# A fused 2-D DFT and squared-ReLU feed-forward kernel: the third TensorE pass of 49 pair steps replaced by arithmetic on VectorE

## The chip, the cores and the metric

The kernel runs on one core of a Trainium2 chip. The metric is device time in microseconds (us), from runs of the whole kernel on the chip; lower is better. The profile is one execution of the kernel, taken by the hardware profiler.

## The reference

For each of 8 batches the real part of a two-dimensional DFT over a 3008 x 256 array is taken, and every one of the resulting 24064 rows goes through a two-layer network with a squared ReLU.

```python
X = np.fft.fft(x, axis=1)          # x: (8, 3008, 256) float32
X = np.fft.fft(X, axis=2)
a = X.real.reshape(24064, 256)
h = np.maximum(a @ w_in, 0.0)      # w_in: (256, 2048)
out = (h * h @ w_out)              # w_out: (2048, 256), float32
```

## The kernel before

The real part of the DFT is a sum of a cosine product and a sine product, and the rows k and S-k of one batch differ only in the sign of the sine product. So the kernel computes one column for each such pair of rows: with P = gh[0]^T zc (cosine) and Q = gh[1]^T zs (sine), the row k has the hidden value P+Q and the row S-k has P-Q. The DFT over the 256 features is folded into the first weight matrix: `gh` holds, for 128 values of d, the cosine part (`gh[:, 0]`), the sine part (`gh[:, 1]`) and the "turn" part (`gh[:, 2]`), all 2048 hidden features wide. Partition 0 of `zs` and of `gh[:, 1]` is used for something else: it holds the row d = 128, which belongs to the cosine product and keeps its sign. `turn2` (L328 to L330) is therefore -2 on partitions 1 to 127 and 0 on partition 0, and `gh[:, 2]` is `gh[:, 1]` times `turn2` (L448): adding gh[2]^T zs to P+Q gives P-Q with the row d = 128 kept.

The 12040 columns are cut into 25 windows w of up to 512 columns (`wins`). Windows 6 to 23 have 512 columns each. In a window there are eight pair steps s = 0 to 7, one for every two groups of 128 hidden features:

- `pq(s)` (L680 to L685): four matmuls of 512 columns, which put P+Q of two groups in a PSUM tile `ph` (two of these tiles exist).
- `square(s, 0)` (L692 to L696): ScalarE takes ReLU of `ph` into an SBUF tile `h1` (three exist), VectorE multiplies it by itself into the left half of `h2`.
- `others(s)` (L698 to L709): the jobs that are spread over the steps. These are 16 matmuls of 256 columns of the second layer for the window before (`part`, L587 to L618, whose PSUM result ScalarE copies to `osb` in every odd step, and the SP queue then stores), the work that prepares later windows, and matmuls that make `zc` and `zs` of the next window (`z_steps`, L458; their last part, `minus` at L494, is on VectorE).
- `turn(s)` (L687 to L690): two matmuls of 512 columns, which add the turn part to the same PSUM tile, so that it then holds P-Q.
- `square(s, 1)`: ReLU and square again, columns reversed, into the right half of `h2`.

The program is written in the order in which each engine is to work: every engine takes its instructions in order. The second layer of window w is done in window w+1: its step s does column group s of `h2`, over all 16 groups of hidden features.

Some windows carry the folding of one more batch of x (`fold_at`): windows 5, 8, 10, 13, 16 and 19. There the steps 0 to 4 each hold one or several VectorE jobs, in this order: `d_even` (L348 to L350), `n_cos` (L358), `d_odd` (L353, after which GpSimd loads the next batch), `n_sin` (L361), `odds` (L368, which writes `od`). In step 5, behind the second layer's matmuls, comes `nyq` (L370 to L375): two tiny TensorE matmuls that read `od`, and a VectorE copy. Step 6 has `even`, step 7 `back`. The windows 6, 9, 12, 15, 18 and 21 (`late_at`) have four smaller VectorE jobs in their steps 2 to 5 (L404, L415).

The loop that orders a window is this:

```python
for s0 in range(0, NST, ng):
    ss = range(s0, s0 + ng)
    for s in ss: pq(s)
    for s in ss: square(s, 0)
    others(s0)
    for s in ss: turn(s)
    for s in ss: square(s, 1)
    for s in ss[1:]: others(s)
```

where `ng` is 1 in all windows but two early ones.

Of the kernel before, what the change touches and what calls it, by code (L numbers as in the profile page):

```python
# [8 lines left out]
F32 = mybir.dt.float32  # L9
F16 = mybir.dt.float16  # L10
I32 = mybir.dt.int32
AF = mybir.ActivationFunctionType
ALU = mybir.AluOpType

HS = 32.0
P = 128
# [3 lines left out]
def rev_dim(ap, i):  # L20

    dims = [list(d) for d in ap.ap]
    step, cnt = dims[i]
    dims[i] = [-step, cnt]
    return bass.AP(tensor=ap.tensor, offset=ap.offset + step * (cnt - 1), ap=dims)
# [3 lines left out]
def kernel(  # L29
# [14 lines left out]
    nc = tc.nc  # L44
    B, S, D = x.shape
    _, F = moe_w_in.shape
# [7 lines left out]
    NFC = F // P  # L54
    WN = 512

    FIRST = [240, 512, 376, 376, 512, 448]
    R23 = float(2.0 ** 23)

    RQ = (1, 3, 5, 0, 2, 4)  # L60

# [11 lines left out]
    wins = []  # L73
# [5 lines left out]
    NW = len(wins)  # L79

    def win_of(col):
        return max(w for w in range(NW) if wins[w][0] <= col) if col < TOT else NW
# [17 lines left out]
    const = ctx.enter_context(tc.tile_pool(name="const", bufs=1))  # L100
    tmp = ctx.enter_context(tc.tile_pool(name="tmp", bufs=2))
# [8 lines left out]
    ps_h = ctx.enter_context(tc.tile_pool(name="ps_h", bufs=2, space=bass.MemoryType.PSUM))  # L110
    ps_o = ctx.enter_context(tc.tile_pool(name="ps_o", bufs=2, space=bass.MemoryType.PSUM))
# [56 lines left out]
    perm = [const.tile([P, P], F16, name=f"perm{i}") for i in range(2)]  # L168
# [3 lines left out]
    nc.gpsimd.memset(idx["c"][0:2, :], P - 3)  # L172
    idx["f"] = iota([P, 1], [[1, 1]], -1, 1, "idx_f")
    nc.gpsimd.memset(idx["f"][0:1, :], 0)
    w16 = [const.tile([P, 2, F // 2], F16, name=f"w16_{i}") for i in range(2)]
    for i in range(2):
        nc.gpsimd.dma_start(out=w16[i], in_=moe_w_in[:, i * F // 2 : (i + 1) * F // 2].rearrange("(c p) f -> p c f", p=P))
    wout16 = const.tile([P, NFC, D], F16, name="wout16")
# [2 lines left out]
    def small(shape, name):  # L181
        return const.tile(shape, F32, name=name)
# [22 lines left out]
    def table_steps(e):  # L205
# [19 lines left out]
        def args(h):  # L225
            t = st["t", h] = tmp.tile([P, 3, NE], F32, name="t", tag="tt")
            for j in range(nr):
                r = row(h, j)
                if e == 0:
                    nc.scalar.activation(t[:, j, 0:n], st["kf"], AF.Copy, bias=R23, scale=vs[:, r : r + 1])  # L230
                else:
                    nc.vector.tensor_scalar(out=t[:, j, 0:n], in0=st["kf"], scalar1=vs[:, r : r + 1], scalar2=R23, op0=ALU.mult, op1=ALU.add)

        def turns(h):
            t = st["t", h]
            nc.vector.tensor_scalar(out=t[:, 0:nr, 0:n], in0=t[:, 0:nr, 0:n], scalar1=-R23, scalar2=-float(S), op0=ALU.add, op1=ALU.mult)

# [44 lines left out]
    at = const.tile([P, 2, P + 1], F32, name="at")  # L282
    for c in range(2):
        nc.scalar.activation(at[:, c, :], drow, AF.Copy, bias=R23, scale=dvs[:, c : c + 1])
    nc.vector.tensor_scalar(out=at, in0=at, scalar1=-R23, scalar2=-float(D), op0=ALU.add, op1=ALU.mult)
    for c in range(2):
# [141 lines left out]
    gh = const.tile([P, 3, F], F16, name="gh")  # L428
# [17 lines left out]
    def gh_turn(cc):  # L446
        f0 = cc * 512
        nc.vector.tensor_scalar(out=gh[:, 2, f0 : f0 + 512], in0=gh[:, 1, f0 : f0 + 512], scalar1=turn2[:, 0:1], scalar2=None, op0=ALU.mult)  # L448
# [3 lines left out]
    def zwin(w):  # L452
        if w not in zc:
            zc[w] = zp.tile([P, WN], F16, name="zc", tag="zc")
            zs[w] = zp.tile([P, WN], F16, name="zs", tag="zs")
        return zc[w], zs[w]
# [101 lines left out]
    for cc in range(1, F // 512):  # L558
        gh_turn(cc)

    def store(osb, p0, g0, m, minus, eng=nc.sync):

        for b, k0, kstep, n, c0 in runs:
            il, ih = max(g0, c0) - c0, min(g0 + m, c0 + n) - 1 - c0
            if minus and k0 in (0, H):
                il = max(il, 1)
            cnt = ih - il + 1
            if cnt <= 0:
                continue
            if minus:  # L570
                lo = p0 + (m - 1) - (c0 + ih - g0)
                row = b * S + S - (k0 + kstep * ih)
            else:
                lo = p0 + c0 + il - g0
                row = b * S + k0 + kstep * il
            eng.dma_start(
                out=bass.AP(tensor=out.tensor, offset=out.offset + row * D, ap=[[kstep * D, cnt], [1, D]]),
                in_=osb[lo : lo + cnt, :])
# [46 lines left out]
    def spread(jobs, i, n):  # L625
        return jobs[len(jobs) * i // n : len(jobs) * (i + 1) // n]
# [3 lines left out]
    def fold_jobs(i):  # L630
        f = folds[i] = fold_steps(i)
        return [f["d_even"], f["n_cos"], f["d_odd"], f["n_sin"], f["odds"], f["nyq"], f["even"], f["back"]]

    fold_at, late_at = {}, {}
    for i in range(2, B):
        fold_at[win_of(col_of[i, 0]) - 2] = i
        late_at[win_of(col_of[i, 1]) - 2] = i
    NST = NFC // 2
    old = None
    for w in range(NW):  # L640
        g0, wn = wins[w]
        h2 = h2p.tile([P, NFC, 2 * WN], F16, name="h2", tag="h2")
        zcw, zsw = zwin(w)

        lo, hi = 0, NST - 1
        at = [[] for _ in range(NST)]
        post = [[] for _ in range(NST)]
        if w == 0:
            at[2] = [f0s["even"], f0s["back"]]
        elif w == 1:  # L650
            fj = fold_jobs(1)
            at = [[f] for f in fj[0:5]] + [[], [], []]
            post[5] = fj[5:6]
            lo, hi = 6, 7
        elif w == 2:
            te = table_steps(1)
            at = [[folds[1]["even"], lambda: te["freq"](), lambda: te["args"](0)], [lambda: te["turns"](0)], [lambda: te["mods"](0)],
                  [lambda: te["absm"](0)], [lambda: te["sins"](0)], [lambda: te["coss"](0)], [], [lambda: te["weigh"]()]]
            for st in range(4):
                at[st + 3] = at[st + 3] + f0s["late"][st : st + 1]  # L660
            at[7].append(folds[1]["back"])
        elif w in fold_at:
            fj = fold_jobs(fold_at[w])
            at = [[f] for f in fj[0:5]] + [[], fj[6:7], fj[7:8]]
            post[5] = fj[5:6]
        elif w == win_of(col_of[1, 1]) - 1:
            for st in range(4):
                at[st] = folds[1]["late"][st : st + 1]
            lo = 4
        if w in late_at:  # L670
            for st in range(4):
                at[st + 2] = at[st + 2] + folds[late_at[w]]["late"][st : st + 1]
        zj, zl = [], []
        for u in need[w + 1]:
            zu = z_steps(u)
            zj += [(zu, 0, 0), (zu, 1, 0), (zu, 0, 1), (zu, 1, 1)]
        f2 = ffn2_steps(*old) if old else []
        phs = {}

        def pq(s):  # L680
            ph = phs[s] = ps_h.tile([P, 2, 512], F32, name="ph", tag="psh")
            for a in range(2):
                f0 = (2 * s + a) * P
                nc.tensor.matmul(ph[:, a, 0:wn], gh[:, 0, f0 : f0 + P], zcw[:, 0:wn], start=True, stop=False)  # L684
                nc.tensor.matmul(ph[:, a, 0:wn], gh[:, 1, f0 : f0 + P], zsw[:, 0:wn], start=False, stop=True)  # L685

        def turn(s):  # L687
            for a in range(2):
                f0 = (2 * s + a) * P
                nc.tensor.matmul(phs[s][:, a, 0:wn], gh[:, 2, f0 : f0 + P], zsw[:, 0:wn], start=False, stop=True, skip_group_check=True)  # L690

        def square(s, sg):  # L692
            h1 = h1p.tile([P, 2, 512], F16, name="h1", tag="h1")
            nc.scalar.activation(h1[:, :, 0:wn], phs[s][:, :, 0:wn], AF.Relu)  # L694
            hv = rev_dim(h1[:, :, 0:wn], 2) if sg else h1[:, :, 0:wn]
            nc.vector.tensor_tensor(h2[:, 2 * s : 2 * s + 2, sg * wn : (sg + 1) * wn], hv, hv, op=ALU.mult)  # L696

        def others(s):  # L698
            for j in at[s]:
                j()  # L700
            for j in spread(f2, s, NST):
                j()
            for j in post[s]:
                j()
            if s == lo:
                zl[:] = [j for zu, part, h in zj for j in zu(part, h)]
            if s >= lo:
                for j in spread(zl, s - lo, hi - lo) if s < hi else []:
                    j()  # L709


        ng = 2 if w == 0 or wins[w - 1][1] < 384 < wn else 1
        for s0 in range(0, NST, ng):
            ss = range(s0, s0 + ng)
            for s in ss:
                pq(s)
            for s in ss:
                square(s, 0)
            others(s0)
            for s in ss:  # L720
                turn(s)
            for s in ss:
                square(s, 1)
            for s in ss[1:]:
                others(s)
        old = (w, h2)
# [32 lines left out]
```

## Time and profile before

| | |
|---|---|
| median of 3 runs | 633.91 us (633.72 to 635.05) |
| span of the profiled execution, first to last instruction | 632.0 us |
| TensorE busy (matmul) | 615.9 us |
| ScalarE busy | 457.4 us |
| VectorE busy | 369.5 us |
| GpSimd busy | 76.5 us |
| granted TensorE clock, mean | 1.000 |
| matmuls of `pq` and `turn` on 512 columns | 3 x 320 |
| VectorE squares on 128 x 1024 (L696) | 320, mean 692 ns |
| ScalarE ReLU on 128 x 1024 (L694) | 320, mean 1026 ns |

"Busy" is the time in which an engine had at least one instruction in work. Matmuls follow each other in a pipeline, so the duration of one (379 ns on 512 columns) is more than the distance between the starts of two. In the table of groups, the last columns give the idle time of the engine just before these instructions and what ended it. The SP queue issues the stores; the GpSimd queue issues the loads of x and of the fold.

### The profile page before, as it was taken

Reading aid. Unit: us, or ns where it says so; the run is one execution under the profiler, and the core shown is the slowest. Engines: PE = TensorE matmul, PEld = TensorE weight load, DVE = VectorE, ACT = ScalarE, POOL = GpSimd, SP = SyncE. Lnnn points to the kernel's source line nnn. Section 1 sums busy time; section 2 is a strip of 40 time slices with the busy share of each in tenths; the row PEclk is TensorE's granted clock in tenths of the full one; section 3 lists DMA queues with packets and bytes.
Section 4 is the critical chain, followed back from the end, with each engine's and each line's share of the span. In section 5 each row is a group of like instructions: output and inputs, shape, how many; then the busy total and the mean of one; then the engine's idle time right before and its main releaser. Section 6 shows DMA issues by size and latency. Waiting matters only on the chain.

```text
span 632.0 us, 11586 instructions
## 1 busy us (share of the span) xinstructions
PE 615.9 (97%) x4548; PEld 439.1 (69%) x4548; DVE 369.5 (58%) x604; ACT 457.4 (72%) x610; POOL 76.5 (12%) x125
## 2 busy tenths in 40 slices
PE   5899999999999999999999999999999999999997
PEld 2457776776777767767777677777677776777786
DVE  7887656765457557645576455854557555454430
ACT  7787778777777677767777777777777777777662
POOL 5352200022002200220011100030000200000000
PEclk9999999999999999999999999999999999999999
DMA  8936211172112711631127211262111311111112
GB/s 146 211 82 127 85 34 34 50 164 78 36 43 58 184 46 42 144 97 35 51 44 160 74 52 39 59 151 73 40 31 55 111 34 47 38 46 35 49 54 65
DMA packets 36525, 47.52 MB, mean 75 GB/s; under 512 B 4216, under 2 KB 30328, under 8 KB 36472
## 3 DMA queue, kind: packets, MB, share of 16 engines
q0 software_dynamic: 9344, 22.14, 17.6%
q1 hardware_dynamic: 26899, 24.44, 12.7%
q8 instruction: 35, 0.57, 0.4%
q10 hardware_dynamic: 228, 0.21, 0.1%
q14 instruction: 19, 0.15, 0.1%
HBM read 33.63 MB, written 27.84 MB: 97 GB/s over the span
## 4 chain that ended last, share of the span: by engine, by line
PE 93%; DVE 3%; ACT 2%; issue 1%; POOL 0%; ACTq 0%; POOLq 0%; DVEq 0%
PE po L596 51%; PE ph L684 12%; PE ph L685 12%; PE ph L690 12%; PE pz L478 4%; ACT h L694 1%; PE pw L301 1%; DVE h L696 1%; PE pg L436 0%; ACT cos L259 0%; DVE fe L349 0%; DVE fo L353 0%; ACT sin L248 0%; ACT gh L440 0%; DVE od L368 0%
## 5 line engine op out<-in xcount | busy, mean ns | idle before, releaser
L694 ACT ACTIVATE h<-ph 128x1024 f16<-128x1024 f32 (+4 forms) x400 | 368.4, 974 | 80.0 <-PE ph L690 72.1
L696 DVE TENSOR_TENSOR h<-h 128x1024 f16<-128x1024 f16 (+4 forms) x400 | 262.4, 660 | 231.6 <-ACT h L694 228.2
L596 PE MATMUL po<-wout,h 128*128 128x256 f16 (+1 forms) x3024 | 361.6, 273 | 0.0
L596 PEld LDWEIGHTS <-h 128*128 128x128 f16 (+1 forms) x3024 | 296.8, 98 | 71.3
L684 PE MATMUL ph<-zc,gh 128*128 128x512 f16 (+4 forms) x400 | 145.9, 366 | 1.1 <-ACT h L694 0.8
L685 PE MATMUL ph<-zs,gh 128*128 128x512 f16 (+4 forms) x400 | 145.9, 366 | 0.4 <-ACT zs L487 0.4
L690 PE MATMUL ph<-zs,gh 128*128 128x512 f16 (+4 forms) x400 | 112.8, 366 | 2.0 <-ACT h L694 1.5
L611 ACT ACTIVATE osb<-po 128x512 f32<-128x512 f32 (+3 forms) x95 | 54.9, 582 | 57.4 <-PE po L596 52.4
L685 PEld LDWEIGHTS <-gh 128*128 128x128 f16 x400 | 39.1, 98 | 43.8 <-issue 2.5
L684 PEld LDWEIGHTS <-gh 128*128 128x128 f16 x400 | 39.0, 98 | 41.8 <-issue 0.5
L690 PEld LDWEIGHTS <-gh 128*128 128x128 f16 x400 | 37.2, 97 | 12.7 <-issue 4.3
L421 POOL COPY xt<-xt 128x2 f16<-128x2 f16 x16 | 2.5, 186 | 173.2 <-DVE xt L404 173.2
L130 POOL DMA_INDIRECT xo<-in_x_dram,idx_r x15 | 22.1, 1471 | 4.6 <-issue 4.6
L125 POOL DMA_DIRECT2D xo<-in_x_dram x8 | 6.0, 751 | 109.8 <-DVE fo L353 109.8
L483 ACT ACTIVATE es<-pz 128x376 f32<-128x376 f32 (+1 forms) x32 | 15.4, 481 | 5.3 <-PE pz L478 5.2
L391 POOL DMA_INDIRECT rb<-scr,idx_r x16 | 18.5, 1158 | 4.9 <-issue 4.9
L487 ACT ACTIVATE zs<-pz 128x376 f16<-128x376 f32 (+23 forms) x27 | 8.5, 358 | 9.9 <-PE pz L478 9.9
L349 DVE TENSOR_TENSOR fe<-xo 128x3072 f16<-128x3072 f16 x8 | 14.3, 1786 | 1.6 <-DMA xo<-in_x_dram,idx_r 1.3
L353 DVE TENSOR_TENSOR fo<-xo 128x3072 f16<-128x3072 f16 x8 | 14.2, 1779 | 0.0
L494 DVE SCALAR_TENSOR_TENSOR zc<-es,pz 128x376 f16<-128x376 f32 (+20 forms) x26 | 9.4, 392 | 7.2 <-ACT zc L487 7.0
L301 PE MATMUL pw<-spn 128*128 128x384 f16 x30 | 8.2, 448 | 5.2 <-DVE spn L290 5.2
L389 POOL DMA_DIRECT2D rb<-scr x16 | 8.8, 551 | 33.4 <-DMA scr<-ev 33.0
(106 smaller groups left out, 220.4 us busy)
## 6 DMA issues: line engine op xcount, KB each, us to landing
out_dram<-osb SPq DMA_DIRECT2D x77, 128.0 KB
xo<-in_x_dram POOLq DMA_DIRECT2D x7, 768.0 KB, 7.0
scr<-ev POOLq DMA_DIRECT2D x8, 390.0 KB, 4.4
rb<-scr POOLq DMA_DIRECT2D x16, 130.0 KB, 5.1
out_dram<-osb SPq DMA_DIRECT2D x12, 94.0 KB
w<-in_moe_w_in_dram POOLq DMA_DIRECT2D x2, 512.0 KB, 10.0
wout<-in_moe_w_out_dram POOLq DMA_DIRECT2D x1, 1024.0 KB, 14.5
out_dram<-osb SPq DMA_DIRECT2D x8, 75.0 KB
```

The costliest lines, as they stand in the source:

```text
L130: nc.gpsimd.indirect_dma_start(out=flat(q), out_offset=None, in_=bass.AP(tensor=x.tensor, offset=0, ap=[[XW, B * S * D // XW], [1, XW]]), ...
L301: nc.tensor.matmul(pw[:, 0 : 3 * P], spn[:, 0, 0, :], spn.rearrange("p c r d -> p (c r d)")[:, 0 : 3 * P], start=True, stop=True)
L391: nc.gpsimd.indirect_dma_start(out=rb[:, q].rearrange("p r d -> p (r d)"), out_offset=None, in_=bass.AP(tensor=src.tensor, offset=src.offs ...
L478: nc.tensor.matmul(ps[:, o0:o1], lhs, tab, start=(h == 0 and k == 0), stop=last, skip_group_check=True)
L483: nc.scalar.activation(es[:, 0:n], ps[:, 0:n], AF.Copy, bias=0.0, scale=1.0)
L596: nc.tensor.matmul(po[0:m, j * D : (j + 1) * D], h2[:, fc, q : q + m], wout16[:, fc, :], start=(fc == 0), stop=(fc == NFC - 1))
L611: nc.scalar.activation(osb[0:mm].rearrange("p s d -> p (s d)")[:, lo:hi], po[0:mm, lo:hi], AF.Copy, bias=0.0, scale=HS * HS)
L684: nc.tensor.matmul(ph[:, a, 0:wn], gh[:, 0, f0 : f0 + P], zcw[:, 0:wn], start=True, stop=False)
L685: nc.tensor.matmul(ph[:, a, 0:wn], gh[:, 1, f0 : f0 + P], zsw[:, 0:wn], start=False, stop=True)
L690: nc.tensor.matmul(phs[s][:, a, 0:wn], gh[:, 2, f0 : f0 + P], zsw[:, 0:wn], start=False, stop=True, skip_group_check=True)
L694: nc.scalar.activation(h1[:, :, 0:wn], phs[s][:, :, 0:wn], AF.Relu)
L696: nc.vector.tensor_tensor(h2[:, 2 * s : 2 * s + 2, sg * wn : (sg + 1) * wn], hv, hv, op=ALU.mult)
```

## The change

In 49 of the pair steps the second pass over `zs` with the turn part is left out. These steps are s = 1, 3 and 5 in windows 6, 7, 9, 11, 12, 14, 15, 17, 18, 20, 21, 22 and 23, and s = 1 and 3 in the fold windows 8, 10, 13, 16 and 19. Such a step runs in another order:

- `half_q(s)`: the two Q matmuls alone; ScalarE copies -2Q into the tile `sn` (two exist, in the space of the weights `w16`, which are no longer used by then); VectorE makes 2 times the d = 128 row's share in two instructions, one for each group of 128 features (`eb`, which has that row of `zs` on all partitions, times `wv`, one number for each hidden feature), and adds it to `sn`.
- `others(s)`, as before.
- `half_p(s)`: the two P matmuls add to the same PSUM tile, which then holds P+Q; ScalarE copies it to the left half of a tile `hd`; VectorE adds `sn` and writes the sum, columns reversed, to the right half; VectorE takes the maximum with 0 over both halves in place, and multiplies both halves with themselves into `h2`.

`row_weights`, in step 0 of window 3, makes `wv` once: 16 matmuls with one column each, which pick partition 0 of `gh[:, 1]`, and a VectorE multiplication by 2. `row_spread(w + 1)`, at the head of step 7 of window w, is a DMA on the SP queue that copies partition 0 of `zs` of the next window to all 128 partitions of `eb` (1 KB each).

```diff
+    MANY, FEW = (1, 3, 5), (1, 3)
...
+    def row_weights():
+        pv = ps_o.tile([P, 512], F32, name="pv", tag="po")
+        for fc in range(NFC):
+            nc.tensor.matmul(pv[:, fc : fc + 1], gh[:, 1, fc * P : (fc + 1) * P], perm[0][:, P - 1 : P], start=True, stop=True)
+        nc.vector.tensor_scalar(out=wv, in0=pv[:, 0:NFC], scalar1=2.0, scalar2=None, op0=ALU.mult)
...
+    def row_spread(w):
+        wn = wins[w][1]
+        t = eb[w] = tmp.tile([P, WN], F16, name="eb", tag="kf")
+        src = zwin(w)[1][0:1, 0:wn]
+        nc.sync.dma_start(out=t[:, 0:wn], in_=bass.AP(tensor=src.tensor, offset=src.offset, ap=[list(src.ap[0]), [0, P], [1, wn]]))
...
+    def halved(w):
+        if wins[w][1] < WN or w < 6:
+            return ()
+        return FEW if w in fold_at else MANY
...
+        if w == 3:
+            at[0].append(row_weights)
...
+        def half_q(s):
+            ph = phs[s] = ps_h.tile([P, 2, 512], F32, name="ph", tag="psh")
+            for a in range(2):
+                f0 = (2 * s + a) * P
+                nc.tensor.matmul(ph[:, a, 0:wn], gh[:, 1, f0 : f0 + P], zsw[:, 0:wn], start=True, stop=True)
+            i = ROT[0] % 2
+            sn = sns[s] = const.tile([P, 2, 2, WN], F16, name=f"sn{i}", tag=f"w16_{i}")
+            nc.scalar.activation(sn[:, 0, :, 0:wn], ph[:, :, 0:wn], AF.Copy, bias=0.0, scale=-2.0)
+            for a in range(2):
+                nc.vector.tensor_scalar(out=sn[:, 1, a, 0:wn], in0=eb[w][:, 0:wn], scalar1=wv[:, 2 * s + a : 2 * s + a + 1], scalar2=None, op0=ALU.mult)
+            nc.vector.tensor_tensor(sn[:, 0, :, 0:wn], sn[:, 0, :, 0:wn], sn[:, 1, :, 0:wn], op=ALU.add)
+
+        def half_p(s):
+            ph, sn = phs[s], sns[s]
+            for a in range(2):
+                f0 = (2 * s + a) * P
+                nc.tensor.matmul(ph[:, a, 0:wn], gh[:, 0, f0 : f0 + P], zcw[:, 0:wn], start=False, stop=True, skip_group_check=True)
+            hd = tmp.tile([P, 2, 2 * WN], F16, name="hd", tag=("tt", "tm")[ROT[0] % 2])
+            ROT[0] += 1
+            nc.scalar.activation(hd[:, :, 0:wn], ph[:, :, 0:wn], AF.Copy, bias=0.0, scale=1.0)
+            nc.vector.tensor_tensor(rev_dim(hd[:, :, wn : 2 * wn], 2), hd[:, :, 0:wn], sn[:, 0, :, 0:wn], op=ALU.add)
+            nc.vector.tensor_scalar(out=hd, in0=hd, scalar1=0.0, scalar2=None, op0=ALU.max)
+            nc.vector.tensor_tensor(h2[:, 2 * s : 2 * s + 2, :], hd, hd, op=ALU.mult)
...
         for s0 in range(0, NST, ng):
             ss = range(s0, s0 + ng)
+            if s0 == hi and w + 1 < NW and halved(w + 1):
+                row_spread(w + 1)
+            if s0 in two:
+                half_q(s0)
+                others(s0)
+                half_p(s0)
+                continue
```

## The prediction

> **What bounds the kernel now.** I read the busy table and the chain of waits first, then the groups by form, then the timeline of a plain step and of a fold window.
>
> ```profile
> PE 615.9 (97%) x4548; PEld 439.1 (69%) x4548; DVE 369.5 (58%) x604; ACT 457.4 (72%) x610; POOL 76.5 (12%) x125
> PE 93%; DVE 3%; ACT 2%; issue 1%; POOL 0%; ACTq 0%; POOLq 0%; DVEq 0%
> L690 PE MATMUL ph<-zs,gh 128*128 128x512 f16 x320 | 94.1, 379 | 0.6 <-ACT h L694 0.5
> L696 DVE TENSOR_TENSOR h<-h 128x1024 f16<-128x1024 f16 x320 | 220.4, 692 | 195.1 <-ACT h L694 195.0
> ```
>
> TensorE has work 97% of the span and is 93% of the chain, so a matmul left out is worth its full distance, as long as nothing makes TensorE wait. VectorE waits for ScalarE 195 us: spare time on average, but I have to look whether it lies where the change needs it.
>
> A plain step without z work (start 302.06) and the next:
>
> ```profile
> 302.06 0.38 PE L684 MATMUL ph<-zc,gh 128*128 128x512 f16 x1
> 302.26 1.94 ACT L694 ACTIVATE h<-ph 128x1024 f16<-128x1024 f32 x2 [1.04 <-PE ph L690]
> 302.28 0.38 PE L685 MATMUL ph<-zs,gh 128*128 128x512 f16 x1
> 304.24 0.69 DVE L696 TENSOR_TENSOR h<-h 128x1024 f16<-128x1024 f16 x1 [0.22 <-ACT h L694]
> 304.68 0.59 PE L690 MATMUL ph<-zs,gh 128*128 128x512 f16 x2
> 305.11 0.38 PE L684 MATMUL ph<-zc,gh 128*128 128x512 f16 x1
> ```
>
> A step is 3.05 us, and two turn matmuls are 305.11 - 304.68 = 0.43 of it (0.215 each; the 379 ns are pipelined). ScalarE does two ReLUs back to back, of the step before and of this one, and ends at step time 2.14; the turn matmuls are due at 2.62.
>
> The fold window 13 (start 317.27, first square of step 0 at 319.50):
>
> ```profile
> 317.27 0.38 PE L684 MATMUL ph<-zc,gh 128*128 128x512 f16 x1
> 319.50 0.69 DVE L696 TENSOR_TENSOR h<-h 128x1024 f16<-128x1024 f16 x1 [0.22 <-ACT h L694]
> 322.14 1.29 DVE L696 TENSOR_TENSOR h<-h 128x1024 f16<-128x1024 f16 x2
> 333.15 0.97 DVE L368 TENSOR_TENSOR od<-ab 128x1548 f16<-128x1548 f16 x1
> 335.93 0.17 PE L373 MATMUL py<-od,perm 128*128 128x1 f16 x1
> ```
>
> `od` is ready at window time 16.85, and TensorE comes to read it, in step 5, at 18.66. These 1.8 us are all the room that VectorE has there, and a TensorE wait for `od` is paid in full.
>
> **Removed.** 49 steps x 2 matmuls x 0.215 = **-21.1 us**, if nothing waits. ScalarE keeps two passes over 128x1024 a step: ReLU 1026 ns, Copy with a scale (L440) 1024 ns.
>
> **Added on VectorE.** A halved step loses two squares and gains six instructions. From these rows:
>
> ```profile
> L448 DVE TENSOR_SCALAR gh<-gh,turn 128x512 f16<-128x512 f16 x4 | 1.2, 349 | 0.0
> L404 DVE TENSOR_TENSOR xt<-rb 128x1040 f16<-128x1040 f16 x16 | 11.1, 694 | 0.0
> L349 DVE TENSOR_TENSOR fe<-xo 128x3072 f16<-128x3072 f16 x8 | 14.3, 1786 | 1.6 <-DMA xo<-in_x_dram,idx_r 1.3
> L245 DVE TENSOR_SCALAR t<-m 128x754 int32<-128x754 int32 x1 | 0.5, 548 | 0.0
> ```
>
> The two `eb` products are L448's form: 0.70. The two additions are a square's size: 1.38. The product over 2048 lies between L404 and L349: 0.694 + 1008 x (1.092/2032) = 1.24. The maximum over 2048 with constants: L448's 512 columns and the same operation on 377 (L265, 0.315) give 0.25 ns a column; L245's 548 less 754 x 0.52 (0.75 at most) leaves 0.15 fixed, so 0.67. Together 4.0; neighbours overlap by some 0.08 (two squares take 1.29), the three that read what the last one wrote don't: **3.9 us** where two packed squares took 1.22. The lower bound, all overlapping, is 3.5. The upper one: no row here writes its columns reversed. Reversed reads run at full rate (L696 reads so in half its cases, median 692 as well); at L442's rate (128x1024, float32 out of PSUM, 1.22) the addition is 0.53 more, and the maximum at half rate, as L245, 0.53 more: 4.95. I take 3.9, as a reversed read is the nearest row.
>
> The Trainium skill (VectorE: DVE Perf Modes, What auto-detection actually checks) lets a 16-bit two-tensor operation run at two columns a cycle for steps of +1 and -1 on every tensor; by it the sum keeps 3.9, and no run yet shows it for a write.
>
> **Fold windows.** VectorE works through: from 2.23, square, `d_even` and square 3.24; step 1: 3.9 + `n_cos` 0.88; step 2: square, `d_odd`, square 2.92; step 3: 3.9 + `n_sin` 0.88; square 0.61 and `odds` 0.97. `od` is ready at 2.23 + 3.24 + 4.78 + 2.92 + 4.78 + 1.58 = **19.5**. TensorE, two halved steps faster, wants it at 18.66 - 0.86 = 17.8. It waits 1.7 us in windows 10, 13, 16 and 19. In window 8, without z matmuls, `nyq` ran at 17.8 and is wanted at 16.95: 2.6. **+9.5 us**; by the bounds 3.5 and 4.95 (ten steps) +5.5 to +20. Queued behind the waiting `nyq` are the z matmuls and the turn of step 5, so all of TensorE; VectorE catches up meanwhile, nothing further is late.
>
> **Windows with three halved steps.** Here no TensorE instruction reads VectorE's work so soon. In the fullest one (four late jobs, 2.0 us), following the same pitches, VectorE ends step 5 at window time 21.7 and the last square of step 7 on time at 25.5: hidden by steps 6 and 7, which are not halved. Three `h1` tiles bind only beyond one and a half steps of lag. At 4.95 it would be 3.2 us late at the end, and the next window's second layer, which needs the last features 2.4 us after its start, would wait some 1.5 to 2.2. I put **+1.0** for edges (13 windows, under 0.1 each).
>
> **P behind ScalarE's copy of Q.** The P matmuls are due at 2.62 - 0.43 = 2.19; the copy ends at 2.14 and a release takes 0.05 to 0.1. The margin of 0.48 is used up: 0 to 0.15 a step, taken 0.03: **+1.5** (0 to 7). z matmuls in a step give 0.15 back.
>
> **Row weights.** 16 single-column matmuls: 0.03 us apart as the two of `nyq`, or 0.11 as second-layer weight loads: 0.5 to 1.8, taken **+1.0**. The VectorE read of `pv` is hidden in window 3.
>
> **The spread DMA.** It waits on the SP queue until `zs` is complete (step 6, some 1.1 us before the next window); behind it wait only that window's last stores. First use is VectorE's in step 1, 4.95 into the window: some 6 us of room, and 8 where the window made no z. The nearest row, 130 KB `rb<-scr`, lands in 5.1: hidden. Bounds: queue q1 moved 26899 packets in 12.7% of 16 engines' span, 48 ns each; 128 packets are 0.4 us over 16 engines and 6.1 on one; so it lands in 5.1 at best and 11 at worst. If late, VectorE stands, and every square behind it.
>
> The Trainium skill (SBUF — State Buffer, Door 1: The DMA port swizzle) speaks against it: one partition reaches one of 16 ports. Its figures would give an estimate of 4.8 us for 128 KB plus a fixed 2, 0.8 more than the room in z windows and then about 1 us more in the sum.
>
> **Sum.** -21.1 + 9.5 + 1.0 + 1.5 + 1.0 = -8.1 from the span of 632.0: 623.9. The median lies 1.9 above that span, so **625.8 us, say 626**.
>
> **Rivals.**
> B, *hardly a wait for `od`*: VectorE's neighbours overlap more. At 3.5 a halved step the wait is 5.5 in all and the sum -12.1, 622; at 3.05 (1.7 less over two steps) it is gone but for window 8, the edges too, and some -19 is left: 615. For it: the overlap seen between squares; against: three instructions of a halved step read what was just written.
> C, *VectorE becomes the bound* (slower): the reversed write runs at L442's rate. From 4.5 us a halved step the gain is gone (each 0.1 costs 1 us in fold windows alone); at 4.95, -8.1 + 10.5 + 13 x 1.5 to 2.2, so +22 to +31: 656 to 665; with the write alone slow (4.4), -8 + 5 + 3 to 8: 634 to 639. For it: no row; against: reversed reads.
> D, *the spread is late*: one engine or one source takes it, 11 us. VectorE would stand 3 to 5 us in 18 windows; fold windows pass on all of it (5 x 4), others half (13 x 2): +38, 672. It decides from some 8 us of landing on.
> That the removed passes were not on the path is excluded by the 0.6 us of idle time before them.
>
> **Numbers.** The forecast, 621 to 631, has 0.53; B 0.14; C 0.27 (two thirds of it at 634 to 645, as other VectorE costs that I missed end there too); D 0.06. The range of 615 to 645 leaves out C's far part and D. Runs of this kernel tell a change from none at about 0.2%, 1.3 us. Faster: forecast, B and a little of C, 0.68; same 0.06; slower 0.26.
>
> **What would show it.** Right: L690 with 302 instructions; in the groups, TensorE waiting for `od` L368 about 2 us at `nyq` in five windows, hardly any wait elsewhere; the six new VectorE rows summing to 4.0. Wrong: an addition of 1.2 us in `half_p`; idle time before the `eb` products put down to a DMA; second-layer matmuls waiting for VectorE.

## The result and the profile after

The changed kernel took 637.84 us (median of 5 runs, 633.93 to 640.29), the kernel before 634.2 (5 runs, 633.72 to 635.05): ratio 1.0053, 95% interval 1.0031 to 1.0075. It is slower, where 625.8 was forecast. The execution that was profiled is the shortest of the five (633.93; span 631.8), so it shows less of the loss than the others had.

The page of the changed kernel, and further down two rows of its view of waits (who waited for whom: us in total, times, longest):

```profile
span 631.8 us, 11651 instructions
PE 599.1 (95%) x4466; PEld 430.7 (68%) x4466; DVE 477.1 (76%) x801; ACT 457.8 (72%) x610; POOL 77.5 (12%) x125
q1 hardware_dynamic: 29491, 26.80, 22.0%
```

The same queue in the kernel before:

```profile
q1 hardware_dynamic: 26899, 24.44, 12.7%
```

The two waits:

```profile
PE py L375 <- DVE od L370: 14.3, 6, 5.9
DVE sn L740 <- DMA eb<-zs: 13.4, 5, 4.2
```

TensorE's busy time fell by 16.8 us, and VectorE's rose by 107.6. TensorE now waits for `od` (1.0 of the 14.3 is the wait of window 1, which was there before), and VectorE waits for the spread row `eb` in five windows. The queue q1 used to take 12.7% of the 16 DMA engines' span; 18 transfers of 128 KB made it 22.0%.

The groups by form of the changed kernel, VectorE's new work:

```profile
L753 DVE TENSOR_TENSOR h<-hd 128x2048 f16<-128x2048 f16 x49 | 60.0, 1225 | 1.7
L752 DVE TENSOR_SCALAR hd<-hd 128x2048 f16<-128x2048 f16 x49 | 34.1, 696 | 1.7
L741 DVE TENSOR_TENSOR sn<-sn 128x1024 f16<-128x1024 f16 x49 | 33.9, 693 | 5.1
L751 DVE TENSOR_TENSOR hd<-hd,sn 128x1024 f16<-128x1024 f16 x49 | 33.7, 689 | 12.6 <-ACT hd L750 11.5
L740 DVE TENSOR_SCALAR sn<-eb,wv 128x512 f16<-128x512 f16 x98 | 30.2, 350 | 13.4 <-DMA eb<-zs 13.4
```

1.225 + 0.696 + 0.693 + 0.689 + 2 x 0.350 = 4.0 us a halved step. The reversed write (L751) runs like the forward addition (L741).

Fold window 8 in the timeline, then the same stretch by windows (the column behind the engines is the granted clock):

```profile
207.60 0.97 DVE L370 TENSOR_TENSOR od<-ab 128x1548 f16<-128x1548 f16 x1
208.62 0.16 PE L375 MATMUL py<-od,perm 128*128 128x1 f16 x1 [2.48 <-DVE od L370]
```

```profile
206.10:209.50 3.40, 0.92 (x6) 0.43 (x5) 3.40 (x5) 0.60 (x1) 0.00 (x0) 0.90 1.08 208
209.50:213.00 3.50, 3.50 (x18) 2.02 (x17) 1.68 (x5) 2.05 (x2) 0.00 (x0) 0.61 1.00 195
213.00:217.00 4.00, 4.00 (x31) 2.78 (x29) 2.33 (x4) 2.31 (x3) 0.61 (x1) 1.00 0.47 147
```

The wait is 2.48 us, as forecast (2.6). What was not in the forecast comes behind it: by the trace's record of the clock, TensorE is at half speed for one stretch of 3.41 us, from 208.81 on. The row of 3.5 us that holds most of it has 18 matmuls, the row of 4.0 us after it 31. That is another 1.7 us lost. In windows 10, 13 and 16 TensorE waits 1.66, 1.66 and 1.62 (1.7 was forecast) and the clock stays. Fold window 19, issue on the SP queue, VectorE, TensorE:

```profile
462.94 4.33 SPq L596 DMA_DIRECT2D out_dram<-osb  x1
467.38 0.49 SPq L579 DMA_DIRECT2D eb<-zs  x1
```

```profile
475.07 0.62 DVE L740 TENSOR_SCALAR sn<-eb,wv 128x512 f16<-128x512 f16 x2 [4.17 <-DMA eb<-zs]
489.18 0.16 PE L375 MATMUL py<-od,perm 128*128 128x1 f16 x1 [5.88 <-DVE od L370]
```

A store holds the SP queue for 4.33 us, the spread is issued behind it, VectorE gets its row 7.7 us after the issue and has stood 4.17 us by then, and the `od` wait is 5.88 where 1.7 was forecast. A half-clock stretch of 3.41 us begins in the last half microsecond of that wait.

I set the starts of the second layer's matmuls of both traces beside each other, window by window. Each of the twelve windows 7, 9, 11 and so on with three halved steps is 1.27 to 1.30 us shorter, window 6 is 0.87 shorter: -16.3. The five fold windows are +3.47, +0.96, +0.96, +0.92 and +6.58 longer: +12.9. The start is 0.5 later, and the last stores end 2.6 later behind the last matmul (not always: 0.5 and 0.6 later in the profiles of e12 and e13, which keep the spread). With 0.2 in windows 2 and 3 these make the difference of the spans, -0.2.

### The profile page after: what moved, and what is told of

The parts are those of the page before. It is cut to its first block, busy times and chain, and to the rows that moved or that the text cites. A ratio compares the mean times of both kernels' runs of the same rounds, so it can differ in the third digit from the quotient of the medians.

```text
span 631.8 us, 11651 instructions
## 1 busy us (share of the span) xinstructions
PE 599.1 (95%) x4466; PEld 430.7 (68%) x4466; DVE 477.1 (76%) x801; ACT 457.8 (72%) x610; POOL 77.5 (12%) x125
## 4 chain that ended last, share of the span: by engine, by line
PE 79%; DVE 9%; issue 3%; DMA 3%; ACT 2%; POOL 2%; ACTq 1%; DVEq 0%; POOLq 0%
PE po L616 45%; PE ph L714 8%; PE ph L715 8%; PE ph L720 8%; PE pz L480 3%; PE ph L747 3%; PE ph L735 3%; DVE h L726 2%; ACT h L724 2%; DMA w<-in_moe_w_in_dram 1%; DVE fo L355 1%; DMA scr<-ev 1%; DVE h L753 1%; DVE od L370 1%; POOL xo L132 1%
## 5 line engine op out<-in xcount | busy, mean ns | idle before, releaser
L724 ACT ACTIVATE h<-ph 128x1024 f16<-128x1024 f32 (+4 forms) x302 | 279.7, 959 | 97.9 <-PE ph L720 87.4
L726 DVE TENSOR_TENSOR h<-h 128x1024 f16<-128x1024 f16 (+4 forms) x302 | 191.4, 647 | 96.3 <-ACT h L724 92.7
L714 PE MATMUL ph<-zc,gh 128*128 128x512 f16 (+4 forms) x302 | 109.8, 365 | 1.1 <-ACT h L724 0.8
L715 PE MATMUL ph<-zs,gh 128*128 128x512 f16 (+4 forms) x302 | 109.7, 365 | 0.6 <-ACT zs L489 0.4
L720 PE MATMUL ph<-zs,gh 128*128 128x512 f16 (+4 forms) x302 | 84.5, 365 | 1.9 <-ACT h L724 1.5
L753 DVE TENSOR_TENSOR h<-hd 128x2048 f16<-128x2048 f16 x49 | 60.0, 1225 | 1.7
L750 ACT ACTIVATE hd<-ph 128x1024 f16<-128x1024 f32 x49 | 50.3, 1026 | 0.2
L738 ACT ACTIVATE sn<-ph 128x1024 f16<-128x1024 f32 x49 | 49.9, 1018 | 0.0
L751 DVE TENSOR_TENSOR hd<-hd,sn 128x1024 f16<-128x1024 f16 x49 | 33.7, 689 | 12.6 <-ACT hd L750 11.5
L740 DVE TENSOR_SCALAR sn<-eb,wv 128x512 f16<-128x512 f16 x98 | 30.2, 350 | 13.4 <-DMA eb<-zs 13.4
L741 DVE TENSOR_TENSOR sn<-sn 128x1024 f16<-128x1024 f16 x49 | 33.9, 693 | 5.1
L752 DVE TENSOR_SCALAR hd<-hd 128x2048 f16<-128x2048 f16 x49 | 34.1, 696 | 1.7
L747 PE MATMUL ph<-zc,gh 128*128 128x512 f16 x98 | 29.1, 378 | 0.0
```

Source lines behind the costliest of these rows:

```text
L738: nc.scalar.activation(sn[:, 0, :, 0:wn], ph[:, :, 0:wn], AF.Copy, bias=0.0, scale=-2.0)
L750: nc.scalar.activation(hd[:, :, 0:wn], ph[:, :, 0:wn], AF.Copy, bias=0.0, scale=1.0)
L753: nc.vector.tensor_tensor(h2[:, 2 * s : 2 * s + 2, :], hd, hd, op=ALU.mult)
```

## The experiments

All ratios are to runs of the kernel before on the same chip; their median lay between 634.3 and 634.9.

| kernel | median us | ratio, 95% interval |
|---|---|---|
| the change | 637.84 | 1.0053 (1.0031 to 1.0075) |
| e1_few0 | 622.47 | 0.980 (0.9782 to 0.9818) |
| e2_nyq7 | 630.69 | 0.9919 (0.9889 to 0.9950) |
| e3_many0 | 646.97 | 1.0195 (1.0178 to 1.0212) |
| e4_fill | 635.6 | 1.0035 (1.0010 to 1.0059) |
| e5_eb0 | 632.56 | 0.9961 (0.9932 to 0.9990) |
| e6_nyq7_eb0 | 624.68 | 0.9859 (0.9817 to 0.9901) |
| e7_nyq7_ebpe | 620.17 | 0.9766 (0.9736 to 0.9796) |
| e8_few0_ebpe | 622.06 | 0.9788 (0.9754 to 0.9822) |
| e9_ebpe | 628.97 | 0.9898 (0.9877 to 0.9919) |
| e10_few15 | 617.77 | 0.9741 (0.9716 to 0.9766) |
| e11_before_spread | 641.04 | 1.0092 (1.0067 to 1.0116) |
| e12_from7 | 632.67 | 0.9972 (0.9956 to 0.9988) |
| e13_from7_few15 | 625.06 | 0.9845 (0.9823 to 0.9867) |

**Where the loss sits: e1 and e3.** Halved steps only outside, or only inside, the fold windows.

```diff
-    MANY, FEW = (1, 3, 5), (1, 3)
+    MANY, FEW = (1, 3, 5), ()        # e1_few0
+    MANY, FEW = (), (1, 3)           # e3_many0
```

> No halved steps in the fold windows: 39 halved steps, 78 matmuls of 0.215 us less. Theory (TensorE's wait for od in the five fold windows, and half-clock stretches of 3.4 us behind such waits, took the gain): no wait at nyq, granted clock 1.000, span 16 us below that of before, time 617 to 619. Rival (every halved step costs something of its own on ScalarE, PSUM or through the spread DMA): the loss stays in proportion, 634 to 638.

> Halved steps in the five fold windows alone (10 steps, 20 matmuls, -4.3 us). Theory: od waits of 1.65 us in four windows and 2.5 in window 8, more where the spread is late, and 1.7 us for each half-clock stretch (two to four): 640 to 648, slower than before. Rival (loss spread over all halved steps): within 1 us of 634 to 635.

e3: 646.97, as expected: its trace has `od` waits of 2.48, 1.66, 1.66, 1.62 and 5.57 and 6.83 us at half clock, two stretches of 3.41, at the last: 13.0 + 3.4 against the 4.3 gained. e1: 622.47, some 4 us short of what I expected. It had no wait for `od` in the fold windows 8 to 19, but windows 6 and 7 were longer than before (+0.9 and +0.4, TensorE waiting 2.04 for `zs`, with a half-clock stretch), window 12 gained only 0.6 and window 18 lost 0.2 (second layer waiting 0.2 and 1.04 for VectorE, behind late spreads). So the fold windows held most of the loss, and not all.

**The od wait and the clock: e2 and e4.**

```diff
-            post[5] = fj[5:6]
+            post[7 if w >= 6 else 5] = fj[5:6]                       # e2_nyq7
...
             py = ps_o.tile([P, 512], F32, name="py", tag="po")
+            for _ in range(9 if i >= 3 else 0):                      # e4_fill
+                nc.tensor.matmul(py[:, P : 4 * P], spn[:, 0, 0, :], spn.rearrange("p c r d -> p (c r d)")[:, 0 : 3 * P], start=True, stop=True)
```

> All 49 halved steps, the two nyq matmuls moved from step 5 to step 7 of the fold windows. Theory: od has been ready for some 3 us when TensorE comes to it, even with a spread that lands 4 us late; no wait, clock 1.000, time 613 to 615. Rival (the cost sits in the halved steps themselves, or in VectorE's load whatever reads od): 630 or more, with VectorE or ScalarE as the releaser of other TensorE waits.

> The changed kernel with nine matmuls of 384 columns on zeros (0.16 us each, 1.44 us) put in front of the nyq matmuls in windows 8, 10, 13, 16 and 19, so that TensorE works while it would wait; their result is overwritten or not read. If the half-clock stretches come from TensorE's idle time: recorded od waits of 0.2 (1.0 in window 8), clock 1.000 or one stretch less per window, time 631 to 634 although no step got shorter. Rival (the stretches are the chip's own and have nothing to do with the wait): clock 0.985 to 0.992 as before, time 637 to 639.

e2 gained 7 us over the change, less than a third of what I expected, and its 630.69 is what the rival said (630 or more). The waits for `od` were gone, and others came, behind late VectorE work: in the profile, which is of the slowest of the four runs (637.12), 4.00 us in window 19 behind a late spread (e13 shows the same) and 3.32 and 1.44 in window 6. e4 ended between its two ranges: 635.6, with a clock of 0.985 to 0.993 in its ten runs, and its interval overlaps that of the change. So its time decides nothing. In its profile, window 8, timeline and then windows:

```profile
206.92 1.63 PE L376 MATMUL py<-spn 128*128 128x384 f16 x9
209.56 0.16 PE L377 MATMUL py<-od,perm 128*128 128x1 f16 x1 [1.02 <-DVE od L370]
```

```profile
207.00:210.40 3.40, 2.38 (x16) 1.24 (x15) 3.40 (x5) 0.76 (x2) 0.00 (x0) 1.00 1.09 208
210.40:213.80 3.40, 3.40 (x26) 2.32 (x24) 2.67 (x5) 2.30 (x3) 0.00 (x0) 1.00 1.02 201
```

The useful work waits as long as in the change, but the clock stays at 1.00. That fits TensorE's idle time as the cause of the stretches and doesn't prove it: whether a given wait is followed by one differs from execution to execution (e3, e5 and e12 had the same 2.48 in window 8, with no filling, and kept their clock). Only window 19, where 4.40 us of wait were left, had 6.83 us at half clock. More weight has the whole set of profiles: behind the start-up and before the last matmul, every stretch begins during a TensorE wait of 2.04 us or more, or within 1.4 us of its end, and e7 and e10, whose longest waits there are 0.94 and 0.25, have none.

**The spread: e5, e6, e7, e8, e9, e11.** e5 and e6 fill `eb` once; e6 has e2's edit too. e7 and e8 put the row on all partitions with one matmul a window; e7 has e2's edit, e8 e1's; e9 is the matmul alone. e11 adds the 18 transfers to the kernel before.

```diff
     def row_spread(w):
         wn = wins[w][1]
+        if w > 6:                                                    # e5, e6
+            eb[w] = eb[6]
+            return
...
-        nc.sync.dma_start(out=t[:, 0:wn], in_=...)
+        pe = ps_o.tile([P, 512], F32, name="pe", tag="po")           # e7, e8, e9; sel: ones in row 0, else zeros
+        nc.tensor.matmul(pe[:, 0:wn], sel, zwin(w)[1][:, 0:wn], start=True, stop=True)
+        nc.scalar.activation(t[:, 0:wn], pe[:, 0:wn], AF.Copy, bias=0.0, scale=1.0)
...
+            if s0 == hi and 6 <= w + 1 < NW - 1:                     # e11, in the kernel before
+                src = zwin(w + 1)[1][0:1, 0:WN]
+                t = tmp.tile([P, WN], F16, name="eb", tag="kf")
+                nc.sync.dma_start(out=t, in_=...)
```

> The changed kernel with the spread done once, for window 6; windows 7 to 23 use that row, so the share of the row d = 128 in the P-Q half of the halved steps is not theirs. Theory (the spread, 128 KB out of one partition, holds all 16 DMA engines for some 5 us, lands late in five windows and makes VectorE, and behind it TensorE, late): no wait of the eb products, the od wait of window 19 falls from 5.9 to 1.7, share of queue q1 back from 22% to 13%, time 624 to 632, with 9 us of od waits still there. Rival (the spread is hidden, od waits and clock alone matter): 635 to 638.

> Both: the nyq matmuls in step 7 and the spread done once, for window 6 (windows 7 to 23 use that row, as in the run before). What is left is VectorE's added work alone. Theory (nothing else costs): waits of TensorE under 3 us in all, clock 1.000 or one stretch, time 613 to 617. Rival (VectorE's load itself makes TensorE late through the h1 tiles in the fold windows): 622 or more.

> All 49 halved steps, nyq matmuls in step 7, and the row d = 128 put on all partitions by one matmul of 512 columns a window (weights: a matrix with ones in row 0) and a ScalarE copy, in step 0, instead of the DMA. 18 x 0.215 = 3.9 us of TensorE is given back, ScalarE has 0.6 us more in a step without a store. Theory: 617 to 621, clock 1.000, no wait of the eb products. Rival (late work on VectorE remains): 625 or more.

> 39 halved steps, none in the fold windows, nyq where it was, the row spread by a matmul in 13 windows (2.8 us). Theory: -16.8 + 2.8 + 0.5 = -13.5: 620 to 622, with the waits that the same kernel with the DMA showed in windows 6, 7, 12 and 18 gone. Rival (those waits are VectorE's own): 622 to 625, no better than with the DMA.

> The changed kernel with the row spread by a matmul and a ScalarE copy in step 0 in place of the DMA; nyq stays in step 5. This is the change with the DMA's own effect taken out: -21.1 + 3.9 + 0.5 and od waits of 1.65 less 0.2 in four windows and 2.5 less 0.2 in window 8, 8.1 us: -8.6, 626, if the clock stays at 1.000; each half-clock stretch behind such a wait adds 1.7 us, so 626 to 634. Rival (the DMA cost little in the median run): 637 or more, as 3.9 us of TensorE are added.

> The kernel before with the 18 spread transfers added and read by nothing: what the transfer costs by itself. Theory (it holds the 16 DMA engines some 5 us, harmful only to what is read soon after): packets of the spread 0.46 us each as in the changed kernel, q1 share 22%, later landing of the fold's transfers, but nothing waits long: 634 to 637. Rival (the transfer slows the kernel whoever reads it): 638 or more.

e9 is the forecast's own sum without the transfer: `od` waits of 2.27, 1.49, 1.50, 1.46 and 1.45, one half-clock stretch behind the first, 628.97 in the median and 626.63 in the one run whose mean clock was 1.000. It is 9 us faster than the change although it adds 3.9 us to TensorE. e7 came out as expected. e8's 622.06 lies where theory and rival meet and isn't told apart from e1's 622.47; in its profile the waits of e1 in windows 6, 7, 12 and 18 are gone (each of them 1.27 to 1.29 shorter than before), as the theory said. e5 ended 0.6 us above my range and e6 8 us above it, inside its rival's (622 or more). The one spread that they keep, for window 6, does harm: windows 6 were 3.94 and 0.87 us longer than before in the profiles, where 1.29 less was due. In e6 that is 2.2 us; 3.7 more were lost in its fold windows, together 0.6 shorter than before where 4.3 was due. e7, which has no spread DMA, shows the same: 0.4 shorter where 3.2 was due. So VectorE's load does cost something there, as the rival had it.

e11 settled what that spread does, against my theory. Nothing reads the 18 transfers, and the kernel is 6.7 us slower. VectorE before, then VectorE, TensorE and windows of e11's profile, in window 6:

```profile
148.85 0.69 DVE L404 TENSOR_TENSOR xt<-rb 128x1040 f16<-128x1040 f16 x1
```

```profile
158.04 0.70 DVE L404 TENSOR_TENSOR xt<-rb 128x1040 f16<-128x1040 f16 x1 [7.86 <-DMA rb<-scr,idx_r]
```

```profile
160.51 1.01 PE L690 MATMUL ph<-zs,gh 128*128 128x512 f16 x2 [4.42 <-ACT h L694]
```

```profile
150.00:158.00 8.00, 6.09 (x42) 3.94 (x41) 0.18 (x1) 3.39 (x4) 1.11 (x2) 1.00 0.27 68
158.00:165.40 7.40, 4.88 (x18) 2.48 (x18) 5.78 (x10) 3.56 (x4) 1.09 (x2) 0.54 0.11 35
```

All of it lies in window 6 (+6.82; every later window 0.0). Its spread is issued at 137.87, just ahead of the fold's round trip through DRAM (`scr`, then `rb`). That takes longer (GpSimd waits 7.26 us for `scr`, 4.40 before), VectorE stands 7.86 us for `rb`, its squares don't free `h1`, ScalarE and then TensorE stand, and 6.83 us at half clock follow. Why the last part of `rb`, issued at 150.44, landed only at 158, with the DMA engines busy 0.27 and 0.11 of the time, the trace doesn't show.

The other profiles with this one spread in them show the same wait, of different lengths. VectorE in the change and in e2:

```profile
152.04 0.70 DVE L406 TENSOR_TENSOR xt<-rb 128x1040 f16<-128x1040 f16 x1 [1.16 <-DMA rb<-scr,idx_r]
```

```profile
160.00 0.70 DVE L406 TENSOR_TENSOR xt<-rb 128x1040 f16<-128x1040 f16 x1 [6.17 <-DMA rb<-scr,idx_r]
```

| profile | wait for `rb` in window 6, us | window 6 against before, us |
|---|---|---|
| the change | 1.16 | -0.87 |
| e4, e6, e1 | 2.87, 2.95, 2.99 | +0.79, +0.87, +0.91 |
| e5 | 5.44 | +3.94 |
| e2 | 6.17 | +4.67 |
| e11 (no halved steps) | 7.86 | +6.82 |

The profiles without that spread have no such wait in window 6 (e3: 0.32).

**The last two: e12 and e13.**

```diff
-        if wins[w][1] < WN or w < 6:
+        if wins[w][1] < WN or w < 7:                                 # e12, e13
-    MANY, FEW = (1, 3, 5), (1, 3)
+    MANY, FEW = (1, 3, 5), (1, 5)                                    # e10, e13, with nyq in step 7; e10 spreads by the matmul
```

> The changed kernel without the halved steps of window 6, and so without the spread that is issued in step 7 of window 5, while the fold's own transfers of that window are under way: 46 halved steps. If that one collision is what makes the changed kernel's usual run slower than its profiled one: window 6 as long as before (24.9 us, -0.87 lost), the usual run 3 to 5 us shorter than the changed kernel's 637.8, 632 to 635, with the od waits of 9 to 14 us still there. Rival (the difference comes from the other 17 spreads or from the clock behind the od waits): 636 to 639.

> Spread by DMA as in the change, but from window 7 on; nyq in step 7; steps 1 and 5 in the fold windows. 46 halved steps, -19.8 + 0.5; no od wait, no collision in window 6. If late spreads are now absorbed by VectorE's free time: 615 to 617, below the kernel that spreads by matmul (617.8), as TensorE is not given 3.9 us back. Rival (the spreads that land late, first in window 19, still reach TensorE through h1 tiles): 619 to 626 and a wider spread of the runs.

> Row spread by a matmul, nyq in step 7, and the halved steps of the fold windows are 1 and 5 instead of 1 and 3. Theory: VectorE's fold jobs in steps 0 to 4 then share with one halved step, the small waits that are left in the fold windows (0.25 to 0.94 us behind h1 tiles) go: fold windows 0.65 shorter than in the kernel before, 2.9 us in all less than with steps 1 and 3: 616.5 to 618. Rival (step 5 pushes the late part over step 7 into the next window): 620 or more, with waits of the second layer for VectorE.

e12 leaves out three halved steps and one spread and is 5.2 us faster than the change. Together with e11 and the table this makes the collision in window 6 the likeliest part of what the profiled execution of the change had been spared; it was not seen in the runs without a profile. e13 has no `od` wait in the fold windows 8 to 19 and still takes 7 us more than e10, which differs in who spreads the row (and in window 6). Its window 19, VectorE and TensorE:

```profile
470.87 0.61 DVE L740 TENSOR_SCALAR sn<-eb,wv 128x512 f16<-128x512 f16 x2 [4.30 <-DMA eb<-zs]
```

```profile
479.81 0.59 PE L720 MATMUL ph<-zs,gh 128*128 128x512 f16 x2 [3.44 <-ACT h L724]
```

So a late spread reaches TensorE in other ways, too, and e13's 625.06 is what its rival said (619 to 626). e10 came out as expected and is the best version, 617.77 us, 2.6% below the kernel before: in its profile every fold window is 0.63 to 0.65 shorter than before, and TensorE waits nowhere behind window 3.

## Why the prediction was wrong

Step by step, by the profile of the change and the runs:

- **Removed**, -21.1: right. Twelve windows gained 1.27 to 1.30 for six matmuls, 6 x 0.215 = 1.29.
- **Added on VectorE**, 4.0 us in durations, reversed write at full rate: right to 0.01. Rival C's premise is excluded; the Trainium skill's rule for steps of -1 (VectorE: DVE Perf Modes, What auto-detection actually checks) holds here for a write, 689 ns against 693 for the forward one.
- **Fold windows**, +9.5: the mechanism, the place and the size were right for four of five (1.66, 1.66, 1.62 and 2.48, against 1.7 and 2.6).
- **Edges, P behind ScalarE's copy, row weights**, +3.5: too much. The rows show no idle time before L747, and the 16 matmuls took 0.5.
- **The spread DMA**, "hidden" with "some 6 us of room", was the step that failed, in three parts: its issue, its landing, and what it delays.
  Its issue: I looked at what waits behind it on the SP queue, not at what stands ahead. In window 19 it was issued 1.2 us after that window's first second-layer matmul, behind a store that held the queue for 4.33 us. The spreads of windows 14, 15, 18, 20 and 21 were issued 3.6 to 3.9 us ahead of that matmul, and their first reader came 7.8 to 7.9 us later without a wait; window 19's row came 7.7 us after its issue, so there the late issue made the 4.2 us, and not a slow landing. Window 11's spread stood behind a store of 8.08 us. The same store as in window 19 stood on the SP queue of the kernel before, just as long, and the sum had nothing for it:

```profile
466.85 4.66 SPq L576 DMA_DIRECT2D out_dram<-osb  x1
```

  Its landing: I took it from the nearest row by size, 5.1 us for 130 KB, whose packets come from many places. Here all 128 come out of one partition. In the packet records of the trace they take 0.46 us each on average, against 0.05 for a store's, and an undisturbed spread (issued at 240.53) moves from 1.21 to 6.07 us after its issue; the five that were late reached VectorE 6.8 to 10.8 us after it. My upper bound of 11 was about right, but I used it for rival D alone, with all 18 late. What happened lies between: five were late (13.4 us of VectorE in all), one of them in a fold window, for 4.2 us.
  What it delays: I had looked only at the spread's own reader, not at the other transfers under way. e11 shows 6.7 us from this alone. That the time ended in rival C's range (634 to 645) is luck of the number: the cause is nearer to D's.
- **Missing**: the clock. A TensorE wait was priced at its length. Of sixteen waits of 2 us and more in the profiles (behind the start-up), twelve came with 3.41 or 6.83 us at half speed, up to 1.7 or 3.4 us more.

By size, in the profiled execution, where the sum of -8.1 became -0.2: 4.2 for the late spread of window 19, an estimate of 3.2 for the two stretches at half clock, 0.4 for window 6; the 2.6 at the end and the 0.5 at the start stand against some 3 of the 3.5 that I put too high. The other four runs took 3.8 to 6.4 us more. Their mean clock was 0.985 to 0.987, against 0.992: over 636 us that is, by estimate, 3 to 4.5 us of TensorE's work, so most of it was time at half clock. That window 6 brought it on is inferred from e2, e5, e11 and e12; how the loss of these four runs divides was not seen run by run.

## What to carry to other kernels

When spare time of one engine pays for another's work, look for the first instruction that reads the busier engine's result early; here moving one pair of tiny matmuls by two steps was worth 8.8 us (e9 against e7), and putting the added work away from the steps that were already full another 2.4 (e7 against e10). Price a new transfer by where its bytes come from, by what stands ahead of it on its queue and by what else is under way then, not by its size; a broadcast out of one partition by a DMA was dearer than a matmul and a copy that do the same (0.2 us of TensorE; e9 is 9 us faster than the change). And price a wait of the matmul engine of some 2 us or more at more than its length.

## What the runs showed of the hardware

- **Half clock behind short waits.** Behind the start-up, waits of TensorE of up to 1.92 us left the clock at 1.00 in every profile here. Of seven waits of 2.00 to 2.48 us, three came with 3.41 us at half speed (2.04 in e1, 2.27 in e9, 2.48 in the change), and four did not. Three of 3.32 to 3.44 us came with 3.41, five of the six of 4.0 us and more with 6.83. The Trainium skill (TensorE: Matmul & The Clock Gate, Part 1: The HAM clock gate) puts the fall to half clock behind an idle window of about 3.4 us; the length of the stretches agrees, but here less idle time was enough.
- **One partition feeds slowly.** 128 KB out of one partition took 4.86 us between the first and the last packet, 27 GB/s, and the 16 DMA engines were busy 0.80 of that time (0.16 over the same time in the kernel before). The Trainium skill (SBUF — State Buffer, Door 1: The DMA port swizzle) says that a partition lies on one of 16 ports; the estimate of 4.8 us from its figures, which the prediction named and did not use, agrees. No run here spread the row from anywhere else, so that the one source is the reason is not shown.
- **A store can hold the queue that issues it.** The median issue on the SP queue took 0.35 us in both kernels, but single ones took up to 5.19 us before and 8.08 us in the change, and what was issued behind them was late by as much. Why just these took so long was not tried.
